# Moving one buffer, sixteen casts and the offsets of a written-out order in a fused attention and expert kernel

## The chip, the cores and the metric

The kernel runs on one core of a Trainium2 chip. The metric is the device time of one execution in microseconds (us). Differences of under 1% are taken as no change in this text.

## The reference

The input is a thresholded attention, a dense feed-forward block and a soft mixture of experts, one after the other. Cut to what matters:

```python
scores = q @ k.T / 8                                  # 4 batches, 8 heads, 576 tokens, head size 64
scores = where(scores >= max(scores) - tau, scores, -1e9)
x = softmax(scores) @ v                               # heads joined: 2304 tokens x 512
g = maximum(x @ w_in, 0) ** 2                         # 2304 x 2048
x = g @ w_out                                         # 2304 x 512
logits = x @ phi                                      # 32 slots
d, c = softmax(logits, axis=0), softmax(logits, axis=1)
s = d.T @ x                                           # 4 slots for each of 8 experts
y[e] = maximum(s[e] @ w1[e], 0) @ w2[e]               # expert width 1024
out = c @ y
```

## The kernel before, in words

**Three bodies of work share the engines.** The attention takes two heads at a time: a pair of heads of one batch is a job, split at first in two, and a job has five query tiles of 128 rows, the last one (mixed) holding the remaining 64 rows of both heads. The weights are converted meanwhile: `w_in` (16 chunks) to two float16 parts, and `w_out` (16 chunks) to 32-bit words that are multiplied with `phi` and stored to memory. The feed-forward runs in nine units of 256 tokens (two for a batch, one for the remainders). After all of it comes a tail with a fixed order: the experts, whose weights are loaded late because their space is that of the attention.

**One query tile.** `s` (TensorE, L688 to L712) makes the scores of two heads; `top` (VectorE, L738) scales them to `u` and takes the bound; `bound` (GpSimd, L744) adds tau; `expo` (ScalarE, L750) makes the exponentials in a tile `e`, both heads in one; `keep` (VectorE, L754) sets what lies below the threshold to zero and sums. In batch 0 and in the mixed tiles TensorE then transposes `e` (`turn`, L275) and ScalarE evacuates it (`p_evac`, L819 and L821). In batches 1 to 3 the full tiles are split in two float16 halves in a tile `hl`: `high` on ScalarE (L773), `low` on GpSimd in four instructions (L777), and a transposing DMA on the SyncE queue (`dturn`, L784) moves `hl` to `pt`. A tile `e` comes free after the last `low` or `turn`, a tile `hl` after its `dturn`. `av` (TensorE, L873 and L881) multiplies with the values.

**One chunk of the weights.** `c_load` brings 128 rows to a slot of `raw64` (eight slots, which later hold q and k of the attention as well). `c_scale` (`head`, L338 on VectorE or L340 on ScalarE) casts the top bytes from bfloat16 to float16; `c_low` (VectorE, L344) makes the low word; `c_shift` (VectorE, L348) joins both and frees the slot. For `w_in` follow a sum of squares, a power of two as the scale, and the halves (`w_hi` L437, `w_lo` L440, `w_times` L445, `w_rest` L450). For `w_out` follow transposes, `c_evac` (L374), `c_prod` (TensorE, L379) and a store. `HDV` says which chunks, by number modulo 4, are cast on VectorE.

**The order is written out by a planner.** `add(kind, engine, cost, ...)` enters each piece with a key; `Plan.run` then plays the kernel through in model time and, on each engine that is free, issues the ready piece of the smallest key. What it issues is the order of the instructions on that engine; an engine later takes them strictly in that order. A key is a due time in planned us (attention and conversion), or 1e5 and a running number (TensorE's pieces of the feed-forward, which therefore fill what the attention leaves), or -1e5 (the feed-forward's pieces on the other engines, which go first). To the key comes an offset for the kind, from `LEAD`. Slots of a buffer are handed out in the order of the keys, too, and the planner knows their number: `EB` of `e`, `HB` of `hl`.

Of the kernel before, what the change touches and what calls it, by code (L numbers as in the profile page):

```python
# [147 lines left out]
def tile_kernel(  # L148
# [31 lines left out]
    RB = 8  # L180
    CB = 4
    GB = 4
    EB = 3
    UB = 4
    PTB = 2
    XPB = 3
    MMB = 4
    QKB = 2
    HB = 2
    WAIT = 0.0  # L190
    DQ = 2.212
    T0 = 10.0
# [4 lines left out]
    TO = 3.4  # L197
    C0 = 2.604
    LOWP = ()
    LEAD = {'c_evac': 8.5, 'c_hi': 109.5, 'c_lo': 76.5, 'c_load': -19.6, 'c_low': 0.2, 'c_out': -17.5, 'c_prod': 65.3, 'c_scale': 13.2, 'c_shift': -19.8, 'c_store': -158.3, 'c_unit': 0.1, 'f_a': 18.2, 'f_acc': 7.3, 'f_alpha': -43.9, 'f_b': -30.4, 'f_cmax': -2.3, 'f_csum': -1.6, 'f_dk': 3.5, 'f_l4': -7.7, 'f_max': 43.7, 'f_merge': 5.1, 'f_p12': -4.1, 'f_pl': 278.3, 'f_pm': -7.7, 'f_relu': 3.3, 'xhi': 3.4, 'xlo': -1.1, 'f_gk': 15.9, 'w_load': 17.8, 'c_turn': 0.0, 'f_sq': -4.5, 'f_p1k': 2.2, 'lphi': -16.2, 'f_turn': 1.5, 'f_p3': -14.5, 'recip': 2.7, 'dturn': -3.1, 'q_scale': -2.9, 'p_evac': -20.3, 'f_total': 0.3, 'w_rest': -1.1, 'av': -1.0, 'r_evac': -3.3, 'w_hi': 6.6, 'w_scale': 0.3, 'v_hi': -6.8, 'top': 3.1, 'eps': -10.6, 'w_diag': -4.8, 'low': -4.3, 'v_scale': -9.2}  # L200
    COST = {('bound', 'POOL'): 0.245, ('c_evac', 'ACT'): 0.493, ('c_low', 'DVE'): 0.35, ('c_low', 'POOL'): 2.12, ('c_out', 'DVE'): 0.104, ('c_scale', 'ACT'): 1.255, ('c_scale', 'DVE'): 0.7, ('c_shift', 'DVE'): 0.61, ('expo', 'ACT'): 0.67, ('f_alpha', 'ACT'): 0.63, ('f_ce', 'ACT'): 0.1, ('f_cmax', 'DVE'): 0.36, ('f_csum', 'DVE'): 0.91, ('f_dk', 'DVE'): 0.22, ('f_gk', 'ACT'): 0.491, ('f_gk', 'DVE'): 0.606, ('f_l4', 'ACT'): 0.279, ('f_max', 'DVE'): 0.33, ('f_merge', 'DVE'): 0.67, ('f_relu', 'ACT'): 0.58, ('f_sq', 'ACT'): 0.525, ('f_sq', 'DVE'): 0.668, ('f_total', 'DVE'): 0.31, ('high', 'ACT'): 0.576, ('keep', 'DVE'): 0.825, ('low', 'POOL'): 0.695, ('q_hi', 'ACT'): 0.73, ('q_lo', 'DVE'): 0.8, ('q_scale', 'DVE'): 0.61, ('q_sq', 'ACT'): 0.82, ('recip', 'DVE'): 0.16, ('spread', 'POOL'): 0.356, ('top', 'DVE'): 0.813, ('v_abs', 'ACT'): 1.2, ('v_hi', 'ACT'): 1.01, ('v_lo', 'DVE'): 1.02, ('w_hi', 'ACT'): 0.612, ('w_lo', 'DVE'): 0.62, ('w_rest', 'POOL'): 1.3, ('w_scale', 'DVE'): 0.6, ('w_sq', 'ACT'): 0.73, ('w_times', 'POOL'): 1.18, ('x_scale', 'DVE'): 0.9, ('xhi', 'ACT'): 0.35, ('xhi', 'DVE'): 0.268, ('xlo', 'DVE'): 0.398}
    PORT = {('w_id', 'POOL'), ('low', 'POOL'), ('w_times', 'POOL'), ('w_rest', 'POOL'), ('spread', 'POOL'), ('c_low', 'POOL'), ('keep', 'DVE'), ('xhi', 'DVE'), ('xlo', 'DVE'), ('c_low', 'DVE'), ('c_shift', 'DVE'), ('w_lo', 'DVE'), ('v_lo', 'DVE'), ('q_lo', 'DVE')}
    FKEY = 1e5
    DTU = (6, 7)
    DEA = (0, 1)
    GKL = (1, 3)
# [5 lines left out]
    DIFD = ()  # L212
    GRAM = True
    QF = 10
    HDV = (0, 2)
    XHA = ()
    QL = 19.2
    LL = 16.0
# [7 lines left out]
    state = {}  # L226
    plan = Plan(
        dict(
            s=1, ma=1, mm=MMB, old=4, u=UB, e=EB, pt=PTB, rp=3, rb=2, rr=2, hl=HB, vh=1, mx=2, xp=XPB, xh=2, xl=1, gt=MC // 2 + 1,
            gk=GB, l4=1, dT=1, qt=QKB, kt=QKB, vraw=2, vbd=2,  # L230
            sm=5, raw64=RB, cv=CB,
        ),
        ("mm", "ma", "xp", "old"),
        WAIT,
        DQ,
    )

    def add(kind, eng, cost, fn, deps=(), key=0.0, *args, **kw):
        cost = COST.get((kind, eng), cost)
        return plan.add(eng, cost, fn, deps, key + LEAD.get(kind, 0.0), *args, port=(kind, eng) in PORT, **kw)  # L240

    def mm_tile(tag="mm"):
        return psp[tag].tile([128, 512], F32, tag=tag, name="mm")
# [722 lines left out]
    def ffn_ops(units):  # L966
# [215 lines left out]

        pending = None
        for n, u in enumerate(units):
            d = dict(gt={}, sq=[], rl=[])
            x = {}
            xdeps = ev_at[u]

            bs = B if u == "rem" else u[0]
            up = scl[:, bs, 1:2]  # L1190

            def xhi(kk, u=u, x=x, up=up):
                if kk == 0:
                    x["x"] = xr if u == "rem" else xp[u]
                    x["h"] = fx.tile([128, KC, NU], F16, tag="xh", name="xh", bufs=2)
                if kk in XHA:
                    nc.scalar.activation(x["h"][:, kk, :], x["x"][:, kk, :], AF.Copy, scale=up)
                else:
                    nc.vector.tensor_scalar(x["h"][:, kk, :], x["x"][:, kk, :], up, None, ALU.mult)

            def xlo(kk, x=x, up=up):
                if kk == 0:
                    x["l"] = fx.tile([128, KC, NU], F16, tag="xl", name="xl", bufs=1)
                nc.vector.scalar_tensor_tensor(
                    x["l"][:, kk, :], x["x"][:, kk, :], up, x["h"][:, kk, :], ALU.mult, ALU.subtract
                )

            hs, ls = [], []
            for kk in range(KC):
                xd = xdeps[kk::KC] + (hs[-1:] if kk else prev.get("hs", [])[-1:] + [xs_op[B if u == "rem" else u[0]]])  # L1210
                h = add("xhi", "ACT" if kk in XHA else "DVE", 0.45 if kk in XHA else 0.2, lambda f=xhi, kk=kk: f(kk), xd, HI, [] if kk else ["xh"])
                l = add("xlo", "DVE", 0.37, lambda f=xlo, kk=kk: f(kk), [h] + ls[:1],
                        HI, [] if kk else ["xl"], [] if u == "rem" else [("xp", xdeps[0])])
                hs.append(h)
                ls.append(l)
            prev["hs"] = hs
            ms = []
            for m2 in range(MC // 2):
                o = {}

                def mm_half(i, m2=m2, x=x, o=o):
                    if i == 0:
                        o["h"] = mm_tile()
                    m = 2 * m2 + i
                    f4, f0 = m * 128 // CW, m * 128 % CW
                    wh, wl = [w_sb[y, f4][:, :, f0:f0 + 128] for y in ("h", "l")]
                    terms = []
                    for kk in range(KC):
                        terms += [(wh[:, kk, :], x["h"][:, kk, :]), (wl[:, kk, :], x["h"][:, kk, :])]
                    for kk in range(KC):  # L1230
                        terms += [(wh[:, kk, :], x["l"][:, kk, :])]
                    for n_, (a, c) in enumerate(terms):
                        nc.tensor.matmul(  # L1233
                            o["h"][:, i * NU:(i + 1) * NU], a, c, start=n_ == 0, stop=n_ == len(terms) - 1
                        )

                f4 = 2 * m2 * 128 // CW
                down = scl[:, bs, 4 + f4:5 + f4]

                def relu(m2=m2, d=d, o=o, down=down):  # L1240
                    g = o["g"] = gt_tile()
                    d.setdefault("pair", {})[m2] = g
                    nc.scalar.activation(g, o["h"], AF.Relu, scale=down)  # L1243
                    d["gt"][2 * m2], d["gt"][2 * m2 + 1] = g[:, 0:NU], g[:, NU:2 * NU]

                def square(m2=m2, o=o, down=down):
                    g = o["g"]
                    if m2 % 4 in SQD:
                        nc.vector.scalar_tensor_tensor(g, o["h"], down, g, ALU.mult, ALU.mult)
                    else:  # L1250
                        nc.scalar.activation(g, g, AF.Square)  # L1251

                a = add("f_a", "PE", 1.31, lambda f=mm_half: f(0), hs + ls + ms[-1:] + (conv_in if n == 0 else []), pk(), ["mm", "gt"])
                b_ = add("f_b", "PE", 1.31, lambda f=mm_half: f(1), [a], pk())
                ms.append(b_)
                dv = m2 % 4 in SQD
                r = add("f_relu", "ACT", 0.49, relu, [b_], HI, [], [] if dv else [("mm", a)])
                s = add("f_sq", "DVE" if dv else "ACT", 0.61 if dv else 0.53, square, [r], HI, rel=[("mm", a)] if dv else [])
                d["rl"].append(a)
                d["sq"].append(s)  # L1260
                if m2 == 0 and pending:
                    pending()
            state["mm"] = ms
            state.setdefault("xl", []).append(ls)
            plan.release(ms[-1], [("xh", hs[0]), ("xl", ls[0])])
            pending = lambda u=u, d=d, n=n: post(u, d, n == 0, n == len(units) - 1, n in DTU)
# [342 lines left out]
```

## Time and profile before

| | before |
|---|---|
| median of 3 runs | 628.82 us (627.69 to 632.64) |
| profiled execution, span from first to last instruction | 624.6 us |
| profiled execution, own time around the span | not recorded by itself; the span is 4.2 us under the median and 3.1 us under the fastest run |
| TensorE busy | 572.8 us (92%) |
| VectorE busy | 449.0 us (72%) |
| ScalarE busy | 447.9 us (72%) |
| GpSimd busy | 286.4 us (46%) |
| DMA moved | 120.97 MB |

PE is TensorE's matmul stream, DVE is VectorE, ACT is ScalarE, POOL is GpSimd and SP is SyncE, whose queue issues nearly all DMAs. L12 is line 12 of the kernel. The shares are means over stages with different limits, so the stages are read one by one.

### The profile page before, as it was taken

To read this page: it belongs to the slowest core of one execution; us is meant where nothing else is said; L and a number is where in the kernel's file an instruction comes from. 1 tells how busy PE (TensorE), PEld (TensorE's weight loads), DVE (VectorE), ACT (ScalarE), POOL (GpSimd) and SP (SyncE) were. 2 spreads that over 40 slices of the span, in tenths; PEclk is the share of its full clock that TensorE was granted. 3 is DMA by queue.
4 is the path that set the end of the run, shared out by engine and by line. 5 is a ranking of instruction groups with operands and counts; after the bars stand their busy time and mean duration, and the time that the engine had idled before them with its cause. 6 is when DMAs were issued, how large, how long until landed. Compare 5 with 4: busy or idle time off the path is not lost. (4 is left out here: it accounts for less than half of the span.)

```text
span 624.6 us, 14082 instructions
## 1 busy us (share of the span) xinstructions
PE 572.8 (92%) x5178; PEld 399.6 (64%) x5178; DVE 449.0 (72%) x1265; ACT 447.9 (72%) x848; POOL 286.4 (46%) x464
## 2 busy tenths in 40 slices
PE   3897979989999999999999989999999999999972
PEld 1454546667677678668757756766777877864321
DVE  5799998999988988887888898878762342342233
ACT  2798666678888988988988878988875857441012
POOL 1455682257667767586756658766750000010000
PEclk9999898999999999999999999999999999999997
DMA  8965525567789676685767655554647799899968
GB/s 274 369 209 189 181 81 186 208 173 202 194 149 195 130 178 108 108 175 123 158 138 138 134 117 104 104 106 95 106 77 233 180 353 225 299 377 387 421 263 302
DMA packets 165940, 120.97 MB, mean 194 GB/s; under 512 B 136560, under 2 KB 145520, under 8 KB 163696
## 3 DMA queue, kind: packets, MB, share of 16 engines
q1 hardware_dynamic: 165296, 117.98, 69.8%
q10 hardware_dynamic: 576, 2.10, 1.1%
q8 instruction: 41, 0.67, 0.4%
q14 instruction: 27, 0.22, 0.1%
HBM read 73.72 MB, written 8.91 MB: 132 GB/s over the span
## 5 line engine op out<-in xcount | busy, mean ns | idle before, releaser
L1233 PEld LDWEIGHTS <-w 128*128 128x128 f16 x1728 | 166.2, 98 | 28.2 <-issue 9.3
L777 POOL TENSOR_TENSOR hl<-e,hl 128x288 f16<-128x288 f32 x192 | 149.2, 800 | 38.0 <-issue 26.8
L1233 PE MATMUL mm<-xh,w 128*128 128x256 f16 x1152 | 149.7, 273 | 0.2 <-ACT gk L1123 0.2
L754 DVE SCALAR_TENSOR_TENSOR e<-u,sm,e 128x576 f32<-128x576 f32 x144 | 122.0, 862 | 18.0 <-ACT e L750 14.4
L750 ACT ACTIVATE e<-u,sm 128x576 f32<-128x576 f32 x144 | 109.2, 771 | 22.1 <-DVE u L738 15.6
L744 POOL TENSOR_SCALAR sm<-sm,tau_p 128x1 f32<-128x1 f32 x144 | 72.8, 511 | 71.9 <-DVE u L738 68.2
L1233 PE MATMUL mm<-xl,w 128*128 128x256 f16 x576 | 86.4, 273 | 0.0
L738 DVE TENSOR_SCALAR_CACHE_REDUCE u<-s,raw 128x576 f32<-128x576 f32 x90 | 71.2, 811 | 13.5 <-PE s L712 12.7
L1243 ACT ACTIVATE gt<-mm,scl 128x512 f32<-128x512 f32 x72 | 49.2, 683 | 42.4 <-PE mm L1233 41.6
L773 ACT ACTIVATE hl<-e 128x576 f16<-128x576 f32 x96 | 64.4, 676 | 2.1 <-DVE e L754 2.0
L841 POOL TENSOR_SCALAR sm<-sm 128x4 f32<-128x4 f32 (+1 forms) x48 | 21.7, 452 | 55.7 <-DVE e L754 47.5
L1251 ACT ACTIVATE gt<-gt 128x512 f32<-128x512 f32 x72 | 45.1, 626 | 1.1
L738 DVE TENSOR_SCALAR_CACHE_REDUCE u<-s,nscale 128x576 f32<-128x576 f32 x54 | 42.6, 808 | 3.4 <-PE s L699 2.8
L1379 POOL MEMSET cv<- 128x512 f32 x4 | 1.9, 525 | 91.2 <-PE mm L1152 91.2
L821 ACT ACTIVATE pt<-mm 128x512 f32<-128x512 f32 x48 | 28.5, 601 | 19.6 <-PE mm L275 19.1
L712 PEld LDWEIGHTS <-qt 128*128 128x128 f16 (+3 forms) x400 | 21.9, 99 | 28.6 <-issue 18.1
L275 PE MATMUL mm<-ident_r,e 128*128 128x128 f32 (+1 forms) x224 | 37.3, 302 | 2.8 <-DVE e L754 2.2
L275 PEld LDWEIGHTS mm<-ident_r,e 128*128 128x128 f32 (+1 forms) x224 | 27.9, 153 | 15.9 <-DVE e L754 5.3
L881 PE MATMUL po<-pt,vh 128*64 128x256 f16 x576 | 36.0, 275 | 0.0
L712 PE MATMUL s<-kt,qt 128*128 128x512 f16 (+1 forms) x200 | 32.9, 289 | 2.4 <-DVE u L738 2.2
L881 PEld LDWEIGHTS <-vh 128*64 128x64 f16 x576 | 29.6, 110 | 5.1 <-issue 4.4
L712 PE MATMUL s<-raw,qt 128*128 128x64 f16 (+1 forms) x200 | 31.2, 293 | 0.0
(205 smaller groups left out, 993.8 us busy)
## 6 DMA issues: line engine op xcount, KB each, us to landing
w<-in_moe_w_dram SPq DMA_DIRECT2D x17, 1024.0 KB, 11.7
w<-in_moe_w_dram SPq DMA_DIRECT2D x22, 512.0 KB, 7.3
raw<-in_moe_w_in_dram SPq DMA_DIRECT2D x16, 511.8 KB, 6.8
raw<-in_moe_w_out_dram SPq DMA_DIRECT2D x16, 511.8 KB, 4.1
raw<-in_v_dram SPq DMA_DIRECT2D x20, 256.0 KB, 3.1
w_out<-cv SPq DMA_DIRECT2D x16, 256.0 KB, 2.7
w<-w_out SPq DMA_DIRECT2D x8, 512.0 KB, 7.9
kt<-in_k_dram SPq DMA_DIRECT2D x10, 320.0 KB, 3.4
```

What stands on the lines that cost most here:

```text
L275: nc.tensor.transpose(out_, in_, ident[:n, :n])
L712: nc.tensor.matmul(o0, d["qh"][r, a, q0], kk, start=full, stop=not full)
L738: nc.vector.tensor_scalar(u, o["s"][:, s0:s0 + S], d.get("nscale", nscale), None, ALU.mult, ALU.min, accum_out=gd["sm"][:, c:c + 1])
L744: nc.gpsimd.tensor_scalar(sm[:, 4 + c:5 + c], sm[:, c:c + 1], tau_p, None, ALU.add)
L750: nc.scalar.activation(e, o["u", a], AF.Exp, scale=-1.0, bias=gd["sm"][:, c:c + 1])
L754: nc.vector.scalar_tensor_tensor(e, o["u", a], sm[:, 4 + c:5 + c], e, ALU.is_le, ALU.mult, accum_out=sm[:, 8 + c:9 + c])
L773: nc.scalar.activation(o["hl"][:, a * S:(a + 1) * S], o["e"][:, a * S:(a + 1) * S], AF.Copy)
L777: nc.gpsimd.tensor_tensor(o["hl"][:, 2 * S:][:, i], o["e"][:, i], o["hl"][:, i], ALU.subtract)
L881: nc.tensor.matmul(po[64 * a:64 * a + 64, :n_], d["vh"][:, y, c0:c0 + D], gd["pt"][:, :, c + 5 * a + m, :], start=i == 0 and m == 0, stop= ...
L1233: nc.tensor.matmul(o["h"][:, i * NU:(i + 1) * NU], a, c, start=n_ == 0, stop=n_ == len(terms) - 1)
L1243: nc.scalar.activation(g, o["h"], AF.Relu, scale=down)
L1251: nc.scalar.activation(g, g, AF.Square)
```

## The change

Four things. The tile `e` has two slots in place of three and the tile `hl` three in place of two (`EB`, `HB`; an `e` is 2 x 576 float32 and an `hl` 4 x 576 float16 for a partition, the same 4,608 bytes). `HDV` becomes empty, so that the 16 casts of chunks 0 and 2 modulo 4 go from VectorE to ScalarE. `LEAD` holds, for each kind, five offsets in place of one: for keys of the attention and conversion the part is chosen by the key (below 40, 76, 140, 270, above), for those of the feed-forward by the unit (0 and 1, 2 and 3, 4 and 5, 6 and 7, 8). And every kind has an entry; before, a kind without one had 0.

```diff
-    EB = 3
+    EB = 2
...
-    HB = 2
+    HB = 3
...
-    LEAD = {..., 'c_load': -19.6, 'c_scale': 13.2, 'c_shift': -19.8, 'c_store': -158.3, 'c_prod': 65.3, 'low': -4.3, 'p_evac': -20.3, 'top': 3.1, 'w_hi': 6.6, 'w_load': 17.8, ...}
+    LEAD = {..., 'bound': (258.1, 112.4, 140.5, 287.5, 198.1), 'c_load': (-21.8, -14.8, -27.8, -22.3, -22.3),
+        'c_prod': (341.5, 355.7, 536.1, 341.5, 341.5), 'c_scale': (365.8, 439.5, 434.8, 428.6, 428.6), 'c_shift': (-136.1, -23.4, -20.8, -18.2, -18.2),
+        'c_store': (-384.9, -310.3, -294.9, -384.9, -384.9), 'expo': (-26.3, -4.4, -3.9, -0.3, -3.9), 'high': (-58.2, -58.2, -169.1, -38, -30.3),
+        'keep': (0.2, -16.5, -41.4, 5.9, -22.1), 'low': (56.7, 56.7, 36.9, -8.9, 9.3), 'p_evac': (-235.8, -169.8, -164.2, -198.9, -211.2),
+        's': (-235.9, -112.8, -100.6, -41.3, 80.4), 'top': (1.6, -0.2, 32.5, 115.1, 230.1), 'turn': (-1.4, 2.4, -1.2, -15.1, -3),
+        'w_hi': (88.2, 213.1, 150.8, 150.8, 150.8), 'w_load': (-150.6, -65.9, -65.9, -65.9, -65.9), ...}
...
+    CUTS = (40.0, 76.0, 140.0, 270.0)
...
-    HDV = (0, 2)
+    HDV = ()
...
     def add(kind, eng, cost, fn, deps=(), key=0.0, *args, **kw):
+        part = state.get("unit", 0) // 2 if abs(key) > FKEY / 2 else sum(key >= c for c in CUTS)
         cost = COST.get((kind, eng), cost)
-        return plan.add(eng, cost, fn, deps, key + LEAD.get(kind, 0.0), *args, port=(kind, eng) in PORT, **kw)
+        return plan.add(eng, cost, fn, deps, key + LEAD[kind][part], *args, port=(kind, eng) in PORT, **kw)
...
         for n, u in enumerate(units):
+            state["unit"] = n
...
                 if m2 == 0 and pending:
+                    state["unit"] = n - 1
                     pending()
+                    state["unit"] = n
```

Of the kinds shown, `bound`, `expo`, `high`, `keep`, `s` and `turn` had no entry before, thus an offset of 0; the diff of `LEAD` is cut to the kinds that the text speaks of.

## Rows read from the trace of the kernel before

**Rows 1.** The page's busy times: engine, busy us (share of span) xinstructions.

```profile
PE 572.8 (92%) x5178; PEld 399.6 (64%) x5178; DVE 449.0 (72%) x1265; ACT 447.9 (72%) x848; POOL 286.4 (46%) x464
```

**Rows 2.** Busy time by stage: stretch, its length, engines (instructions), clock, DMA share, GB/s.

```profile
core 0: us, PE busy (x) PEld busy (x) DVE busy (x) ACT busy (x) POOL busy (x), PEclk, DMA share, GB/s
0.00:16.00 16.00, 5.12 (x22) 2.38 (x22) 9.05 (x25) 4.57 (x4) 2.05 (x8) 1.00 0.88 275
16.00:144.00 128.00, 111.75 (x735) 72.13 (x733) 118.26 (x316) 96.09 (x180) 65.95 (x109) 0.95 0.59 199
144.00:300.00 156.00, 153.01 (x1522) 113.74 (x1522) 132.32 (x379) 137.24 (x268) 105.21 (x171) 1.00 0.74 155
300.00:477.00 177.00, 172.31 (x1763) 126.90 (x1767) 140.33 (x405) 147.91 (x295) 111.30 (x174) 1.00 0.59 115
477.00:560.00 83.00, 83.00 (x771) 64.64 (x772) 28.78 (x86) 50.64 (x79) 1.15 (x3) 1.00 0.95 293
560.00:625.00 65.00, 47.62 (x379) 19.75 (x378) 20.22 (x56) 11.49 (x24) 0.77 (x2) 0.94 0.87 343
```

**Rows 3.** The feed-forward's first matmuls: first and last start of L1233.

```profile
L1233 PEld LDWEIGHTS <-w x1728: 95/98/181, 144.1 to 548.9; 128*128 128x128 f16 x192
```

**Rows 4.** The chain that ended last, near its end: start, us, what.

```profile
566.45 8.87 DMA w<-in_moe_w_dram
...
591.62 13.82 DMA w<-in_moe_w_dram
```

**Rows 5.** The second stage by halves, columns as in Rows 2.

```profile
96.00:144.00 48.00, 44.95 (x342) 31.36 (x340) 45.01 (x124) 35.49 (x69) 19.41 (x36) 0.97 0.62 197
16.00:96.00 80.00, 66.80 (x395) 40.77 (x394) 73.25 (x193) 60.59 (x112) 46.55 (x74) 0.93 0.58 200
```

**Rows 6.** Groups by line from 16 to 144 us: the casts on both engines.

```profile
L338 DVE CAST raw<-raw 128x512 f16<-128x512 bf16 x13 | 12.3, 1004 | 0.0
...
L340 ACT ACTIVATE raw<-raw 128x512 f16<-128x512 bf16 x13 | 17.5, 1367 | 3.9 <-DMA raw<-in_moe_w_in_dram 3.8
```

**Rows 7.** Casts on VectorE, whole run: ns min/median/max, first and last start.

```profile
L338 DVE CAST raw<-raw x16: 716/962/1223, 6.1 to 134.1; 128x512 f16<-128x512 bf16 x16
```

**Rows 8.** One stretch in which both engines are nearly full, columns as in Rows 2.

```profile
32.00:48.00 16.00, 14.56 (x105) 9.15 (x101) 15.96 (x44) 15.26 (x27) 7.52 (x13) 1.00 0.71 226
```

**Rows 9.** ScalarE's waits from 16 to 144 us: total, times, longest.

```profile
ACT pt L821 <- PE mm L275: 14.0, 13, 2.9
ACT e L750 <- DVE u L738: 10.6, 11, 2.6
```

**Rows 10.** SyncE's queue waits from 0 to 144 us.

```profile
SPq L328 <- DVE gt L348: 17.2, 8, 7.0
...
SPq L328 <- DVE cv L348: 10.0, 5, 3.7
```

**Rows 11.** VectorE's waits from 144 to 477 us.

```profile
DVE e L754 <- ACT e L750: 12.7, 13, 2.3
DVE u L738 <- PE s L712: 12.7, 15, 2.4
...
DVE e L754 <- POOL sm L744: 1.4, 2, 1.2
```

**Rows 12.** ScalarE's waits from 144 to 477 us, on a slot of e.

```profile
ACT e L750 <- POOL hl L777: 5.8, 7, 1.2
```

**Rows 13.** The page's group of `high`: count, busy us, mean ns, idle before it.

```profile
L773 ACT ACTIVATE hl<-e 128x576 f16<-128x576 f32 x96 | 64.4, 676 | 2.1 <-DVE e L754 2.0
```

**Rows 14.** Exponentials on ScalarE in order of time, 325 to 338 us.

```profile
325.40 2.11 ACT L750 ACTIVATE e<-u,sm 128x576 f32<-128x576 f32 x3
...
337.80 0.78 ACT L750 ACTIVATE e<-u,sm 128x576 f32<-128x576 f32 x1 [0.89 <-POOL hl L777]
```

**Rows 15.** The low halves on GpSimd that end before that wait does.

```profile
335.83 1.93 POOL L777 TENSOR_TENSOR hl<-e,hl 128x288 f16<-128x288 f32 x2
```

**Rows 16.** Exponentials alone, from 144 to 477 us: ScalarE's busy time (count).

```profile
144.00:477.00 333.00, 76.95 (x102) 1.00 0.66 134
```

More of the change, by code (lines that the diff above doesn't have):

```diff
@@ L199, in tile_kernel @@
     LOWP = ()
-    LEAD = {'c_evac': 8.5, 'c_hi': 109.5, 'c_lo': 76.5, 'c_load': -19.6, 'c_low': 0.2, 'c_out': -17.5, 'c_prod': 65.3, 'c_scale': 13.2, 'c_shift': -19.8, 'c_store': -158.3, 'c_unit': 0.1, 'f_a': 18.2, 'f_acc': 7.3, 'f_alpha': -43.9, 'f_b': -30.4, 'f_cmax': -2.3, 'f_csum': -1.6, 'f_dk': 3.5, 'f_l4': -7.7, 'f_max': 43.7, 'f_merge': 5.1, 'f_p12': -4.1, 'f_pl': 278.3, 'f_pm': -7.7, 'f_relu': 3.3, 'xhi': 3.4, 'xlo': -1.1, 'f_gk': 15.9, 'w_load': 17.8, 'c_turn': 0.0, 'f_sq': -4.5, 'f_p1k': 2.2, 'lphi': -16.2, 'f_turn': 1.5, 'f_p3': -14.5, 'recip': 2.7, 'dturn': -3.1, 'q_scale': -2.9, 'p_evac': -20.3, 'f_total': 0.3, 'w_rest': -1.1, 'av': -1.0, 'r_evac': -3.3, 'w_hi': 6.6, 'w_scale': 0.3, 'v_hi': -6.8, 'top': 3.1, 'eps': -10.6, 'w_diag': -4.8, 'low': -4.3, 'v_scale': -9.2}
+    LEAD = {'av': (-39.9, -201.1, -174.8, -18.8, -189), 'bound': (258.1, 112.4, 140.5, 287.5, 198.1), 'c_evac': (11.5, -89.5, 120.8, 11.5, 11.5), 'c_load': (-21.8, -14.8, -27.8, -22.3, -22.3), 'c_low': (-1.5, 18.7, 133.5, -7.5, -7.5), 'c_out': (-159.4, -327.9, -194.5, -159.4, -159.4), 'c_prod': (341.5, 355.7, 536.1, 341.5, 341.5), 'c_scale': (365.8, 439.5, 434.8, 428.6, 428.6), 'c_shift': (-136.1, -23.4, -20.8, -18.2, -18.2), 'c_store': (-384.9, -310.3, -294.9, -384.9, -384.9), 'c_turn': (231.8, 192.1, 205.8, 231.8, 231.8), 'dturn': (-10.2, -10.2, -4.2, -6.4, 0.7), 'eps': (-626.1, -502.4, -261.4, -393.2, -255.9), 'evac': (-77.1, -19.9, 22, 139.3, -12.1), 'expo': (-26.3, -4.4, -3.9, -0.3, -3.9), 'f_a': (7.8, 6.9, 23.1, 41.2, 89), 'f_acc': (-276.5, -296.9, -213.2, -146.5, -275.4), 'f_alpha': (-602.5, -515.5, -483.8, -422.7, -76.4), 'f_b': (-125.8, -77, -228.2, -133, -296.8), 'f_ce': (-104.1, 31.6, 194.8, -70.2, -51.7), 'f_cmax': (-126.9, -47.4, -46.2, -43.8, -141), 'f_csum': (-234.9, -316.1, -218.1, -318.2, -291), 'f_dk': (-284, -64.4, -203.4, -120, -336.3), 'f_gk': (9.1, 294.1, 275.1, 214, 244.5), 'f_join': (-51.5, -51.5, -51.5, -45.8, -51.5), 'f_l4': (-397.3, -67.8, -66.5, -42.1, -20.2), 'f_max': (-400.7, -191.3, -819.6, -249.3, -148.6), 'f_merge': (-401.4, 1.2, -16.5, -187.8, -104.5), 'f_move': (-140.2, -140.2, -140.2, -27.2, -140.2), 'f_p12': (-118.8, -176.5, -178.2, -109.4, 57.8), 'f_p1k': (-236.9, -89, 29.2, -104.8, -16.8), 'f_p3': (-0.2, -45.9, -83.4, -120.5, -169.1), 'f_part': (114.6, 114.6, 114.6, 67.3, 114.6), 'f_pl': (517.2, 640, 442.6, 609.1, 978.5), 'f_pm': (-145.9, -119.5, -256.7, -269.5, -365.2), 'f_relu': (-579.7, -542.5, -295, -397.7, -407), 'f_rs': (71.6, 71.6, 71.6, 71.6, 71.5), 'f_sq': (-94.2, -365, -232, 26.3, -376.2), 'f_total': (-4, -245.1, -106.5, 40.6, 52.4), 'f_turn': (-2.1, -21.1, -29.4, 1.6, 132.3), 'high': (-58.2, -58.2, -169.1, -38, -30.3), 'keep': (0.2, -16.5, -41.4, 5.9, -22.1), 'low': (56.7, 56.7, 36.9, -8.9, 9.3), 'lphi': (17.6, 136.4, 17.6, 17.6, 17.6), 'lraw': (-4.9, 9.5, -0.4, -15.5, -35.4), 'lrem': (4.1, 8.1, 152.7, 102.3, 8.1), 'p_evac': (-235.8, -169.8, -164.2, -198.9, -211.2), 'q_hi': (5, 5, 25.2, -330.6, -32.6), 'q_lo': (-255.4, -255.4, -344.9, -394, -415.2), 'q_move': (-7.2, -7.2, 3.4, -12, -203.6), 'q_scale': (47.4, 47.4, 121, 60.3, 68.1), 'q_sq': (10.7, 10.7, -7.8, -5.1, 43.9), 'q_sum': (56.2, 56.2, 126.3, 98.1, 189.9), 'r_evac': (-193.2, -7.7, -0.1, -222.8, -338.8), 'r_turn': (0.5, 10.2, 0.6, 0, -14.8), 'recip': (2.8, 23.2, 22.6, 19, 120.7), 's': (-235.9, -112.8, -100.6, -41.3, 80.4), 'spread': (-255, -205.5, -97.5, -72, -87.9), 'top': (1.6, -0.2, 32.5, 115.1, 230.1), 'turn': (-1.4, 2.4, -1.2, -15.1, -3), 'v_abs': (-209.1, -285.9, -263.8, -252.1, -59.2), 'v_hi': (-83.2, -83.2, -187.7, -76.2, -60), 'v_lo': (48.8, 48.8, -23.3, 40.6, -25.8), 'v_scale': (-324.1, 18.8, 167.6, 154.4, -357.5), 'v_sum': (114.3, 33.4, -3.2, -58.2, 105.3), 'w_diag': (-50.6, 57, -133.5, -133.5, -133.5), 'w_diff': (-239.1, 106.3, -87.2, -87.2, -87.2), 'w_gram': (32.9, 167.2, 114.6, 114.6, 114.6), 'w_hi': (88.2, 213.1, 150.8, 150.8, 150.8), 'w_id': (489.7, 302.5, 300.7, 300.7, 300.7), 'w_lo': (1.9, -92, 2.7, 2.7, 2.7), 'w_load': (-150.6, -65.9, -65.9, -65.9, -65.9), 'w_pre': (-38.2, 48.9, 48.9, 48.9, 48.9), 'w_rest': (-152.8, 140.9, -37, -37, -37), 'w_round': (196.1, 340.5, 184.3, 184.3, 184.3), 'w_scale': (-0.3, -21, 2.8, 2.8, 2.8), 'w_sum': (137.6, 169.3, 100.1, 100.1, 100.1), 'w_times': (321.3, 378.5, 230.8, 230.8, 230.8), 'w_wide': (20.4, 20.4, 20.4, 20.4, -133.3), 'x_scale': (-148.5, -136.7, -136.7, -162.1, -151), 'xhi': (107.7, 211.3, 220.4, 267.9, 289.8), 'xlo': (-181.3, -127.3, -13.1, 15.2, 54.9)}
```

## The prediction

> **What bounds the kernel now.** I read the page's busy line first: TensorE is busy for 572.8 of 624.6 us [rows 1]. The change takes no matmul away and adds none, so it can only shorten the roughly 52 us in which TensorE stands idle. The table by stage shows where they are [rows 2]. From 0 to 16 us: 10.9 idle, while the first data arrive. From 16 to 144: 128 - 111.75 = 16.3 idle. From 144 to 477: 333 - 325.3 = 7.7 idle. From 477 to 560: none. From 560 on: 17.4 idle, in a tail whose order is not planned.
>
> The stage from 16 to 144 us has no filler: the feed-forward's first matmul starts at 144.1 [rows 3]. VectorE is full there, 118.26 of 128 us (92%), and ScalarE is not, 96.09 (75%). The halves of that stage say where filler would help: 13.2 us of TensorE's idle time lie before 96 us, 3 after [rows 5]. From 144 to 477 TensorE is 98% busy, VectorE 82% and ScalarE 86% [rows 2]. After the attention, at 477, the expert weights stream in: the DMA share is 0.95 up to 560, and the chain that ended last consists of those loads from 566 to 605 [rows 2, 4]. So an earlier end pays only if the attention ends earlier (its space is then loaded into) and TensorE's work is denser; both move together where the first stage gets shorter.
>
> The sum is made against the profiled execution, span 624.6 us. Its time around the span is not known; the span stands 4.2 us under the median 628.82, and I apply the difference to the median.
>
> **Part 1, the casts.** In the stage from 16 to 144 us VectorE has 13 of them for 12.3 us, and 13 on ScalarE cost 17.5 [rows 6]; the other three of VectorE's 16 lie before 16 us, where both engines wait for data. Moved, VectorE has 118.3 - 12.3 = 106.0 and ScalarE 96.1 + 17.5 = 113.6. The good end: VectorE stays the limit at its share of 92.4%, 106.0 / 0.924 = 114.7, so 13.3 us are gained. The bad end: ScalarE becomes the limit at the best share that it has over a long stage, 137.24 / 156 = 88% [rows 2], so 113.6 / 0.88 = 129.1, a loss of 1.1. Between them lies the one stretch where both are nearly full, with ScalarE at 15.26 of 16 us, 95.4% [rows 8]: 113.6 / 0.954 = 119.1, a gain of 8.9. I take 4, the middle of 8.9 and -1.1, because that stretch is only 16 us long. A cast takes 1.37 us and its key is now 366 to 440 behind its due time, so that any attention piece that is ready goes ahead of it; it has to fit in ScalarE's gaps, and the two largest, waits for a transpose and for `u`, sum to 24.6 us in 24 pieces of at most 2.9 [rows 9]. Thirteen casts need 17.5 of that, but a cast that has begun holds up an exponential by up to 1.37.
>
> The row says that a cast costs 0.95 us as a median on VectorE, up to 1.22, against 1.37 on ScalarE [rows 6, 7]. The Trainium skill, Perfetto Trace Analysis, section Optimizing Scalar/DVE Operations, says that VectorE is the faster one where it has a performance mode, and that moving work to ScalarE may pay when VectorE is saturated. By its first half the stage loses 17.5 - 12.3 = 5.2 us of engine time and the time would be 634; by the second, with VectorE at 92%, it gains the full 13.3. The rows carry both, as ends above and as rivals below.
>
> What is queued behind a late cast: `c_shift` waits for it, and with it the slot of `raw64`. SyncE's queue already stands 27.2 us for such slots [rows 10], and the q, k and v loads are behind those on the queue. The loads' own offsets differ by 2 to 8 us from before, so I cost them at nothing: the feed-forward does not need the weights before 144.
>
> **Part 2, the slots.** No row shows ScalarE idle for a slot of `hl`: `high` has 2.1 us of idle time before it in 96 instructions, 2.0 of them for `keep` [rows 13]. So the third `hl` is worth 0 by itself; at most it lets the planner issue what it held back. The third `e` is used: exponentials wait 5.8 us, 7 times, for the last `low` of an older tile [rows 12]. One such case: the tile whose `low` ends at 335.83 + 1.93 = 337.76 had its first exponential at about 326.8 at the latest (the third of three from 325.40), so it held its slot 11 us [rows 14, 15]. What two slots allow: 102 exponentials from 144 to 477 us [rows 16] are 102 x 80 / 144 = 57 tiles (64 tiles of two heads and 16 of one make 144), one in 333 / 57 = 5.84 us, so two slots do as long as a slot is held for under 11.7 us on average. That is close. Ends: 0, and the rival below. I take 0 loss, because the new offsets shorten the hold: in the later parts `keep` goes before `top` (-41 to 6 against 32 to 230), `high` before `expo`, and `low` before `bound` on GpSimd.
>
> **Part 3, the offsets.** What differs most on TensorE is `s`, which now goes 41 to 236 us ahead of its old place up to key 270. VectorE waits 12.7 us for scores and 12.7 for exponentials between 144 and 477 [rows 11]; earlier scores take from the first. The added wait is `bound` behind up to four `low`, on which `keep` waits; it costs 1.4 us now [rows 11]. Only TensorE's idle 7.7 us can come back here; ends 7.7 and, for a worse fit of the plan to the chip, a loss of the same size. I take a gain of 4, about half, since the scores are the largest of these waits and the work that fills TensorE is unchanged. On SyncE's queue stores of `w_out` go still earlier and `w_load` by 168; the stage that they load in is 95% full, so 0. The first 16 us and the tail: 0; their cover is the data's arrival and the stream of loads.
>
> **Sum.** -4 - 4 = -8 from the span, 616.6, and 621 for the median.
>
> **The rivals.** (a) All comes back: VectorE alone limits the first stage (-13.3) and all of 7.7 us is refilled: 628.8 - 21 = 608. For it: ScalarE's gaps are long enough in sum. Against: they are in 24 pieces, and 95% is the most that it ever shows.
>
> (b) ScalarE takes VectorE's place and the gain is given back: +1.1 and nothing from the offsets, 630. For it: 113.6 us of work in a stage that must then be under 120 long; and the 5.2 us of added engine time, in full and uncovered, would give 634. Against: casts of `w_out` need not be done before 144, and ScalarE has 14% free after that.
>
> (c) The two `e` slots limit the attention between 144 and 477: it decides from a mean hold of 11.7 us. At 12.4, 0.7 above, a tile takes 6.2 us in place of 5.84, so the attention ends 57 x 0.36 = 20 us later. TensorE fills with feed-forward, but the loads start later; of their 128 us from 477 to 605 about 5%, 6 us, are free. The end moves by 14, less the 4 of part 1: 639. For it: the hold of 11 us read above and the waits that three slots already show. Against: `keep`, `high` and `low` now come first.
>
> **How the numbers follow.** My forecast has 0.43, (a) 0.11, (b) 0.25, (c) 0.15; the other 0.06 are mishaps and windfalls that I can't name. The forecast's own range is 612 to 628 (part 1 from 8.9 to 0, part 3 from 7.7 to 0, with something left over). The range from 608 to 637 leaves out the outer half of (a), most of (c) and the unnamed. Within 1% is what a measurement here can't tell from no change: 622.5 to 635.1. Faster by more: 0.36 of the forecast's 0.43, (a) and 0.03, so 0.50. Slower: (c), a fifth of (b) and 0.02, so 0.22. Same: the rest, 0.28.
>
> **What would show it.** Part 1: in the stage before the feed-forward, VectorE loses 12 us, ScalarE gains 17 to 18, and the feed-forward's first matmul starts at about 140 or earlier; if it starts after 144, or ScalarE's share there is above 95% while VectorE's falls under 85%, (b) is right. Part 2: exponentials that wait for `low` for well over 5.8 us in total, and an attention that ends after 477, are (c). Part 3: VectorE's wait for scores falls under 12.7 and TensorE's idle time in the attention stage under 7.7. The forecast is wrong if the first stage is as long as before, or if it is shorter and the loads at the end start no earlier.

## The result and the profile after

The changed kernel takes 612.66 us (median of 4 runs, 610.26 to 613.72) against 628.3 us: a ratio of 0.9743, 95% interval 0.9709 to 0.9778. The forecast was 621, so the direction was right and the gain, 15.6 us, is twice the one forecast. Here and below, medians and ratios leave out disturbed, slower executions.

The profiled execution took 610.26 us with a span of 608.5, so 1.8 us lie around the span. By that the profiled execution of before, span 624.6, stood near 626.4, about 2 us under its median, and not 4.2 as the prediction took it.

First the page's busy times of the changed kernel (columns as in [rows 1]).

```profile
PE 566.6 (93%) x5178; PEld 396.2 (65%) x5178; DVE 437.5 (72%) x1249; ACT 463.4 (76%) x864; POOL 280.6 (46%) x464
```

VectorE lost 11.5 us and ScalarE gained 15.5: in the main the casts. TensorE has the same 5178 matmuls, but is busy for 6.2 us less than in [rows 1]. Its idle time is 608.5 - 566.6 = 41.9 us, against 51.8: so 9.9 us of the 16.1 that the span lost were idle time, and 6.2 are shorter busy time of the same matmuls. The stages of the changed kernel (columns as in [rows 2]):

```profile
0.00:16.00 16.00, 5.45 (x24) 2.70 (x24) 8.06 (x23) 9.22 (x7) 2.06 (x8) 1.00 0.88 299
16.00:96.00 80.00, 73.42 (x499) 47.22 (x498) 76.66 (x212) 77.42 (x139) 46.06 (x73) 1.00 0.71 242
96.00:144.00 48.00, 45.54 (x349) 32.34 (x347) 43.84 (x124) 39.59 (x75) 30.40 (x50) 0.96 0.65 190
144.00:300.00 156.00, 153.24 (x1543) 112.88 (x1542) 132.05 (x376) 136.81 (x269) 100.26 (x170) 1.00 0.73 146
300.00:477.00 177.00, 174.07 (x1763) 130.60 (x1764) 129.89 (x380) 148.69 (x290) 99.91 (x161) 1.00 0.64 132
477.00:560.00 83.00, 82.65 (x762) 56.76 (x763) 32.28 (x98) 42.88 (x72) 1.92 (x4) 1.00 1.01 306
560.00:609.00 49.00, 32.23 (x252) 13.74 (x244) 14.73 (x39) 8.83 (x18) 0.00 (x0) 0.92 0.82 328
```

The row to read is the second, against the second of [rows 5]. From 16 to 96 us TensorE now does 499 matmuls in place of 395 and is idle for 6.6 us in place of 13.2; VectorE is 96% busy (92% before) and ScalarE 97% (76% before). From 144 to 477 TensorE's idle time goes from 7.7 to 5.7 us [rows 2]. TensorE's idle time in the other stages moved by under 1 us each. Next the first feed-forward matmul, and the chain near its end (start, us, what):

```profile
L1237 PEld LDWEIGHTS <-w x1728: 95/98/181, 150.3 to 534.7; 128*128 128x128 f16 x192
```

```profile
559.19 16.23 DMA w<-in_moe_w_dram
575.44 13.81 DMA w<-in_moe_w_dram
```

The feed-forward starts 6 us later than in [rows 3] and ends 14 us earlier (534.7 against 548.9), and the loads at the end of the chain finish at 589.25 and not at 605.44 [rows 4]. The mark that the prediction set, a first feed-forward matmul at 140 or earlier, did not come true: the stage without the feed-forward got 6 us longer, and more attention was done in it. The attention's last matmul starts at 458.3 us, 476.7 before. By 150 us ScalarE had run 49 exponentials, 44 before (one row each, first the changed kernel, the line's instructions from 0 to 150 us; share of DMA and GB/s last):

```profile
0.00:150.00 150.00, 38.11 (x49) 0.99 0.71 230
```

```profile
0.00:150.00 150.00, 33.83 (x44) 0.95 0.64 210
```

The waits that the prediction spoke of, from 144 to 477 us in the changed kernel, VectorE's and then ScalarE's (total, times, longest):

```profile
DVE u L741 <- PE s L715: 13.5, 16, 2.3
...
DVE e L757 <- POOL sm L747: 5.8, 8, 1.4
```

```profile
ACT e L753 <- POOL hl L780: 3.8, 5, 2.3
```

VectorE's wait for scores did not fall (12.7 in [rows 11]); the added wait behind `bound` is there, 5.8 us against 1.4; and exponentials wait less for a slot of `e` with two slots than they did with three (5.8 in [rows 12]).

### The profile page after: what moved, and what is told of

It is laid out like the page before. It is cut to its first block, busy times and chain, and to the rows that moved or that the text cites. A ratio compares the mean times of both kernels' runs of the same rounds, so it can differ in the third digit from the quotient of the medians.

```text
span 608.5 us, 14103 instructions
## 1 busy us (share of the span) xinstructions
PE 566.6 (93%) x5178; PEld 396.2 (65%) x5178; DVE 437.5 (72%) x1249; ACT 463.4 (76%) x864; POOL 280.6 (46%) x464
## 4 chain that ended last, share of the span: by engine, by line
PE 36%; DMA 8%; DVE 7%; ACT 2%; issue 2%; POOL 1%; DVEq 0%; ACTq 0%; POOLq 0%; SPq 0%
PE mm L1237 21%; DMA w<-in_moe_w_dram 8%; PE mm L278 3%; PE s L715 3%; PE po L884 3%; PE mm L990 2%; DVE e L757 2%; PE mm L1155 1%; DVE u L741 1%; POOL hl L780 1%; PE po L889 1%; DVE ob L1529 1%; DVE raw L643 1%; DVE xl L1208 0%; PE mm L997 0%
## 5 line engine op out<-in xcount | busy, mean ns | idle before, releaser
L780 POOL TENSOR_TENSOR hl<-e,hl 128x288 f16<-128x288 f32 x192 | 145.9, 784 | 44.3 <-ACT hl L776 32.7
L757 DVE SCALAR_TENSOR_TENSOR e<-u,sm,e 128x576 f32<-128x576 f32 x144 | 119.3, 849 | 13.8 <-POOL sm L747 8.3
L747 POOL TENSOR_SCALAR sm<-sm,tau_p 128x1 f32<-128x1 f32 x144 | 71.1, 500 | 68.1 <-DVE u L741 64.5
L741 DVE TENSOR_SCALAR_CACHE_REDUCE u<-s,raw 128x576 f32<-128x576 f32 x90 | 71.1, 810 | 13.8 <-PE s L715 13.5
L343 ACT ACTIVATE raw<-raw 128x512 f16<-128x512 bf16 x32 | 42.8, 1388 | 5.6 <-DMA raw<-in_moe_w_in_dram 5.6
L844 POOL TENSOR_SCALAR sm<-sm 128x4 f32<-128x4 f32 (+1 forms) x48 | 19.8, 413 | 40.9 <-DVE e L757 37.7
L278 PEld LDWEIGHTS mm<-ident_r,e 128*128 128x128 f32 (+1 forms) x224 | 25.3, 142 | 18.1 <-issue 6.5
L278 PE MATMUL mm<-ident_r,e 128*128 128x128 f32 (+1 forms) x224 | 34.8, 285 | 2.0 <-DVE e L757 1.2
```

Source lines behind the costliest of these rows:

```text
L278: nc.tensor.transpose(out_, in_, ident[:n, :n])
L741: nc.vector.tensor_scalar(u, o["s"][:, s0:s0 + S], d.get("nscale", nscale), None, ALU.mult, ALU.min, accum_out=gd["sm"][:, c:c + 1])
L747: nc.gpsimd.tensor_scalar(sm[:, 4 + c:5 + c], sm[:, c:c + 1], tau_p, None, ALU.add)
L757: nc.vector.scalar_tensor_tensor(e, o["u", a], sm[:, 4 + c:5 + c], e, ALU.is_le, ALU.mult, accum_out=sm[:, 8 + c:9 + c])
L780: nc.gpsimd.tensor_tensor(o["hl"][:, 2 * S:][:, i], o["e"][:, i], o["hl"][:, i], ALU.subtract)
```

## The experiments

The theories at the start: A, the new offsets make an order that keeps ScalarE and VectorE full at once before 100 us, and the casts and slots only make room for it; B, taking the casts off VectorE is itself the gain; C, the slots are. Each part by itself first.

**Casts alone.**

```diff
  (the kernel before)
-    HDV = (0, 2)
+    HDV = ()
```

> The kernel before with the 16 casts moved to ScalarE, old offsets and old slots, the order planned anew. Theory A (the gain of 16 us is made before 100 us, by an order that keeps ScalarE and VectorE full at once; the casts only make room): within 4 us of the kernel before, 624 to 632, ScalarE's share from 16 to 96 us between 85 and 92%. Theory B (taking the casts off VectorE, the limit, is itself the gain): 616 to 621, with 7 to 11 us gone from the first 100 us. Theory C (the slots make it): no change, 626 to 630.

Measured: 630.26 us, ratio to before 1.0033 (0.9997 to 1.007). No gain. From 16 to 96 us of this run, from 48 to 96, and its page's busy times:

```profile
16.00:96.00 80.00, 70.12 (x446) 44.28 (x447) 73.07 (x202) 76.07 (x133) 46.87 (x78) 0.98 0.66 228
48.00:96.00 48.00, 42.81 (x305) 27.35 (x303) 45.43 (x126) 47.56 (x81) 31.24 (x52) 1.00 0.51 169
PE 580.9 (92%) x5178; PEld 403.0 (64%) x5178; DVE 437.0 (69%) x1249; ACT 464.4 (74%) x864; POOL 279.1 (44%) x464
```

Theory A's time came out; its share did not: from 16 to 96 us ScalarE is 95% busy (99% from 48 on), VectorE 91%. TensorE idles for 9.9 us there (13.2 before), and the feed-forward starts at 141.2 us, 3 us earlier. Over the whole span of 630.7 us its idle time is 49.8, only 2.0 less than before, while its busy time is 8.1 longer, at a clock of 0.973 (0.983 before). So the time is that of rival (b), 630, but (b)'s marks are not there: the feed-forward is not late, and VectorE is not under 85%. The Trainium skill, Perfetto Trace Analysis, section Optimizing Scalar/DVE Operations, holds that moving work to ScalarE may pay when VectorE is saturated; here, at 92%, it did not by itself.

**Slots alone, and both.**

```diff
  (the kernel before; the second run with HDV = () as well)
-    EB = 3
+    EB = 2
-    HB = 2
+    HB = 3
```

> The kernel before with two slots of e and three of hl, old offsets and casts. Theories A and B: 626 to 636, since exponentials then wait longer for a slot (over 5.8 us from 144 to 477). Theory C: 622 or less.

> Both, with the old offsets: the whole change but for the offsets. Theory A: 622 to 634, so that the new offsets are worth at least 10 us. Theory B: 615 to 621. Theory C: under 620.

Measured: 630.72 us, ratio 1.0046 (1.0021 to 1.0071), and 628.06 us, ratio 0.9981 (0.9951 to 1.001). All of the change but the offsets is worth nothing. B and C fall; on top of it the offsets are worth 628.06 - 612.66 = 15.4 us (12.6 by a second measurement of the changed kernel, 615.46 us, at the end of this section). With the slots alone exponentials did not wait longer for a slot of `e`, as A and B had it, but for 3.2 us from 144 to 477 (5.8 in [rows 12]). Where the old offsets leave the early stage, from 16 to 48 and from 48 to 96 us of the run with both:

```profile
16.00:48.00 32.00, 25.86 (x150) 15.51 (x150) 29.40 (x82) 30.15 (x55) 16.23 (x26) 1.00 0.91 326
48.00:96.00 48.00, 41.30 (x279) 27.16 (x280) 41.39 (x115) 44.82 (x76) 26.58 (x46) 0.93 0.50 171
```

TensorE idles for 6.1 and 6.7 us there, 12.8 together, against 6.6 with the new offsets. The new offsets without the casts or with the old slots were not tried: the planner finds no order with them. Three slots of both tiles do not fit the memory.

**The new order, with the casts on VectorE.** The order stays; only the engine of 16 instructions is changed.

```diff
  (the changed kernel)
-                if top == "DVE":
+                if n % 4 in (0, 2):
```

> The changed kernel in its own written-out order, but the 16 casts of chunks 0 and 2 modulo 4 run on VectorE at the place in its queue where the order has them. VectorE gets back about 11 us of work before 96 us, where it is 96% busy, and ScalarE loses 14 to 16 us. Theory A with both engines as limits, and theory B: 8 to 13 us slower than the changed kernel, 620 to 626. If the order alone counts and the engine of a cast does not: 612 to 616.

Measured: 621.16 us, ratio 0.988 (0.9839 to 0.9921). Inside the new order the move of the casts is worth 8.5 us (5.7 against 615.46), inside the old one nothing. The order was planned for the casts on ScalarE; for VectorE the planner finds none with the new offsets. From 16 to 96 us, and to 144:

```profile
16.00:96.00 80.00, 70.13 (x481) 43.93 (x480) 78.34 (x211) 65.09 (x124) 47.72 (x71) 1.00 0.66 230
96.00:144.00 48.00, 42.26 (x305) 29.06 (x305) 45.99 (x126) 34.75 (x65) 28.91 (x44) 0.97 0.64 199
```

VectorE is 98% full, ScalarE 81%, and TensorE idles for 9.9 and 5.7 us where the changed kernel has 6.6 and 2.5: one full engine sets the pace as long as the other is not used.

**Which offsets.** Theory A1: the conversion's, with the casts going last. A2: the attention's own. One group put back to the old values in each run, and in the third the casts' alone.

```diff
  (the changed kernel; three runs)
-    LEAD = {...}
+    LEAD = {..., every kind c_*, w_* and lphi: its one old offset five times}   # first
+    LEAD = {..., every kind of the attention: its one old offset five times}    # second
+    LEAD = {..., 'c_scale': (13.2, 13.2, 13.2, 13.2, 13.2)}                     # third
```

> The changed kernel with the old offsets for the kinds of the weights' conversion (c_ and w_, and phi's load), the new ones for attention and feed-forward. Theory A1 (what fills ScalarE and VectorE early is that the conversion, the casts above all, goes last and fits in gaps): 622 to 630. Theory A2 (the attention's own new offsets, scores first and finished tiles first, make it): 612 to 617.

> The changed kernel with the old offsets for the attention's kinds, the new ones for conversion and feed-forward. Theory A1: 612 to 618. Theory A2: 622 to 632. If neither works without the other: over 620 here and over 620 with the old offsets of the conversion.

> The changed kernel with one offset undone, that of the casts (13.2 as before, in place of 366 to 440), so that a cast goes when it is due and not behind all attention. Theory A1 in its narrow form (the casts' place at the end of ScalarE's choice): 618 to 626, with exponentials later in the first 100 us. If the casts' place does not count: 611 to 615.

Measured: 635.97 us, ratio 1.0144 (1.0119 to 1.0169); 626.02 us, ratio 0.9974 (0.9948 to 1.0001); 632.87 us, ratio 1.0105 (1.0057 to 1.0152). Each takes the whole gain away; the first and the third are slower than any theory here had them. In the first TensorE's idle time is 60.9 us (51.8 before), in the third it is 52.3, as before, and the run's clock is 0.972. That neither group works without the other is what the expectation named for it, but one kind's offset costing as much as a whole group is suspect: it may be that any touch does it.

**Any touch.** All large differences between kinds stay; every offset but those of eight kinds (`top`, `keep`, `turn` and five others) is shifted at random by up to 1 us (twice) and by up to 3.

```diff
  (the changed kernel)
-    LEAD = {..., 'c_scale': (365.8, 439.5, ...), ...}
+    LEAD = {..., each value + uniform(-1, 1) or uniform(-3, 3), ...}
```

> The changed kernel with every offset (but for eight kinds with which the planner finds no order) shifted by a random amount of up to 1 us, which leaves all the large differences between kinds as they are, but gives another written-out order. Theory P (the gain is in what the offsets say on the whole: casts last, scores first): 611 to 618. Theory O (the gain belongs to the one order that these offsets happen to give): 620 to 640, like the runs in which one group of offsets was undone.

> The same with other random shifts of up to 1 us, to see the spread between such orders. Theory P: 611 to 618. Theory O: 620 to 640, and more than 4 us away from the first.

> The same with random shifts of up to 3 us. Theory P: 611 to 620, no farther off than with 1 us. Theory O: 620 to 640, no better and no worse than with 1 us, since any shift gives just another order.

Measured: ratios 0.999 (0.9936 to 1.0043), 1.0003 (0.9972 to 1.0034) and 1.0038 (1.0005 to 1.0071), with medians 626.71, 628.36 and 629.65 us. The gain is gone in all three, with 3 us no more than with 1. (The second is 1.7 us from the first, where theory O expected over 4.) The clock is not the reason: TensorE's idle time is 53.4, 52.0 and 51.8 us, against 41.9; and at clocks of 0.984 to 0.987 four executions of the first took 624.9 to 626.7 us, the changed kernel at 0.983 to 0.986 took 612.4 to 613.7. So theory P falls and O is left: in these three orders, what the offsets say on the whole (casts last, scores first) is worth nothing by itself; the gain belongs to the one order that the changed kernel's values give. And the runs that undid one group say less than they seem to, since a shift that means nothing costs as much. From 16 to 96 us the first two of the three are between before and after, with TensorE idle for 8.9 and 9.1 us:

```profile
16.00:96.00 80.00, 71.10 (x474) 44.50 (x473) 74.24 (x203) 74.40 (x134) 45.55 (x78) 0.98 0.62 214
16.00:96.00 80.00, 70.86 (x472) 44.98 (x472) 74.10 (x211) 77.28 (x138) 41.10 (x72) 0.94 0.67 226
```

**The third slot of hl.** Once planned with two, once with the order of the changed kernel kept and only two slots in memory.

```diff
  (the changed kernel, planned anew)
-    HB = 3
+    HB = 2
  (the changed kernel, same order)
-                        o["hl"] = at.tile([128, 4 * S], F16, tag="hl", name="hl", bufs=HB)
+                        o["hl"] = at.tile([128, 4 * S], F16, tag="hl", name="hl", bufs=2)
```

> The changed kernel with two slots of hl in place of three, two of e, order planned anew. By the prediction's part 2 (no row shows anything waiting for a slot of hl): 611 to 615. If the third slot is what the new order lives on between 144 and 460 us: over 617, with the attention's end later than 458 us.

> The changed kernel in its own order, planned with three slots of hl, but with only two in memory, so that a tile's halves wait for the transposing DMA of the tile two before. If nothing waits for a slot of hl, as part 2 of the prediction had it: 611 to 615. If the third slot carries the new order between 144 and 460 us: over 618, with ScalarE waiting there in front of the first half (L776) for that DMA, and the attention's end later than 458 us.

Measured: 646.83 us, ratio 1.0315 (1.0289 to 1.0342), and 637.1 us, ratio 1.0122 (1.0059 to 1.0184). In the same order the slot is worth 637.1 - 612.66 = 24 us (21.6 against 615.46). In the profiles TensorE's idle time is 15.7 us longer, 57.6 against 41.9, and its busy time 12.8, at a clock of 0.970 against 0.991. The first halves of this run, with what ScalarE waits for in front of them, and its stage from 144 us:

```profile
  DMA pt<-hl: 27.8, 12
```

```profile
144.00:300.00 156.00, 142.92 (x1326) 103.63 (x1326) 116.50 (x326) 120.09 (x236) 86.92 (x149) 0.93 0.62 129
```

ScalarE stands 27.8 us, 12 times, until the transposing DMA has freed a slot; TensorE is idle for 13.1 us there where the changed kernel has 2.8. In [rows 13] nothing waits for a slot: the planner issues a first half only when a slot is free in its own time (`fits`), so the old order, planned with two, holds it back. The run planned anew with two shows it: its first halves wait for a slot for only 2.3 us, and it is the slowest of all. (Both runs have four slots of `e` and `hl` together, the kernel before five.) Both runs have the changed kernel's early stage (TensorE idles for 6.5 and 7.2 us from 16 to 96 us), and their attention's last matmul starts at 499.0 and 487.4 us: the early stage alone does not make the gain.

**Where in the order.** The order is kept up to a planned time, and from there all offsets (again but for eight kinds) are shifted by up to 1 us (other random values in each run), so that another order follows; the third run is the changed kernel beside them.

```diff
  (the changed kernel, in Plan.run)
+            if self.now >= 150.0 and not getattr(self, 'moved', False):   # or 320.0
+                self.moved = True
+                ...   # each piece that is not issued yet gets its key with the shifted offset
```

> The changed kernel's order up to planned 150 us; from there every offset (but for eight kinds) shifted by up to 1 us, so that another order follows. Theory E (the gain is made before 150 us, where 6 heads more are done and 7 us of idle time are gone): it is kept, 611 to 617. Theory W (the order has to fit to the end, an early lead is lost again in the attention's later part): 620 to 630, with the same first 150 us as the changed kernel and the attention ending after 460 us.

> The same with the order kept up to planned 320 us. Theory E: 611 to 617. Theory W: between the changed kernel and the run kept to 150, 614 to 624, with the loss after 320 us alone.

> The changed kernel itself, for a comparison on the same chip: 610 to 615 by every theory, 2 to 3% under the kernel before.

Measured: kept to 150, 622.36 us, ratio 0.9893 (0.9862 to 0.9924); kept to 320, 616.12 us, ratio 0.9804 (0.9747 to 0.986); the changed kernel 615.46 us, ratio 0.9784 (0.9734 to 0.9834). The runs of before beside them have 628.9. So of 13.4 us, 6.5 are left with the order kept to 150 us and 12.8 with it kept to 320: half, and nearly all. E falls; both times lie where W had them. From 300 to 460 us of the run kept to 150, of the one kept to 320, and of the kernel before:

```profile
300.00:460.00 160.00, 150.95 (x1490) 111.27 (x1488) 124.99 (x366) 130.81 (x262) 97.06 (x164) 0.96 0.61 115
```

```profile
300.00:460.00 160.00, 155.99 (x1574) 114.67 (x1572) 128.38 (x382) 135.86 (x275) 100.06 (x164) 0.99 0.61 117
```

```profile
300.00:460.00 160.00, 155.53 (x1571) 114.38 (x1572) 132.69 (x382) 136.32 (x271) 105.39 (x167) 1.00 0.61 118
```

TensorE's idle time is 9.1 us in the first, 4.0 in the second and 4.5 before. So a part of the early lead is lost again there when the order changes at 150: the idle time of that run's whole span is 48.5 us, 3.3 less than before, though 6.4 had been saved by 144 us. The second half needs its own good order. Each rests on one set of shifts; other sets could land elsewhere.

## Why the prediction was right and wrong

**The step that failed is part 3, the offsets.** It said: "Only TensorE's idle 7.7 us can come back here", that is between 144 and 477 us, and took 4. Measured, the offsets are worth 15.4 us with casts and slots in place (12.6 by the second measurement), and most of the idle time that came back lies where part 3 did not look: TensorE's idle time fell by 6.6 us from 16 to 96 and by only 2.0 from 144 to 477, and without the new offsets those 6.6 are not there (12.8 us idle against 13.2). Its reason failed too: the wait for scores went from 12.7 to 13.5 us, and in the three shifted runs the direction of the offsets alone did nothing.

**Part 1, the casts, was wrong in its size.** It took 4 for the casts by themselves; alone they gave no time that can be told from none (630.26 us), and 2 us of idle time. The bound that limited ScalarE to 95.4% at best was too low: in the new order it is 97% busy over 80 us. The casts count with the order: 8.5 us go when they are taken back out of the new order. Its marks misled as well. From 16 to 144 us VectorE did not lose 12 us but was filled with other work (120.5 us, 118.3 before). By the feed-forward's start, 150.3 us, the forecast's own sign of being wrong and one of rival (b)'s signs came true, while the gain was twice the forecast: a start that moves says little where the order decides what is done before it. What held is that the end moves with the loads behind the attention: they finish 16.2 us earlier, and the span is 16.1 shorter.

**Part 2, the slots, was wrong on hl.** "The third `hl` is worth 0 by itself" holds in the old order (the slots alone gave a ratio of 1.0046) and fails in the new one, where it carries 24 us. The step that failed is from "nothing waits for it" to "worth 0": a planned order shows no wait for a resource that it was planned around. On `e` it was right: rival (c) did not come, and the waits fell.

**A step left out.** "It can only shorten the roughly 52 us in which TensorE stands idle" held only for the idle time, 9.9 us against the 8 forecast. The other 6.2 us of the span are TensorE's busy time, and most of them go with the clock. The profiled run of the changed kernel had a mean granted clock of 0.991, before 0.983. A second profile of the changed kernel, at 0.980, has a span of 613.6 us, and its page says:

```profile
PE 571.4 (93%) x5178; PEld 400.2 (65%) x5178; DVE 437.9 (71%) x1249; ACT 463.5 (76%) x864; POOL 279.4 (46%) x464
```

Its idle time is 613.6 - 571.4 = 42.2 us, as in the first; its matmuls took 4.8 us longer. Against before, with nearly the same clock, the span is 11.0 us shorter, 9.6 of it idle time. The profile of before was about 2 us under its own median, so that the medians differ by more. That the clock makes only a small part of the gain is shown by executions of one clock beside each other: at 0.980 the changed kernel had spans of 613.6 to 613.9 us, and the kernel before 626.9 and 627.7. How much of the clock comes with the order stays open: over all runs here, the changed kernel has a mean of 0.984 (8 runs) and before 0.981 (76 runs).

**The sum.** The idle time in all, 9.9 us, came out near the 8 of the forecast by luck, for the terms did not: 4, 0 and 4 were taken for casts, slots and offsets. By themselves the first two give nothing, and the offsets, with the others in place, 15.4 us of time.

What stays open: why this order is the good one, beyond that it keeps VectorE and ScalarE at 96 and 97% before 96 us and TensorE's idle time low after. Shares nearly as high, 93 and 97%, stand in the second shifted order, which has no gain, so they are not shown to be the cause. No single rule in it was shown to carry the gain.

## What to carry to other kernels

Where a planner writes out the order, an engine's or a buffer's worth is that of the order built on it: test a part inside the new order, without changing the order, and not only in the old one. A trace without a wait for a buffer does not say that one more buffer is worth nothing, since the plan may have held the work back. And before an offset is explained, shift all of them by an amount that means nothing: if that takes the gain away, the gain belongs to the one order and not to the reason.

## What the runs showed of the hardware

The same order of the same kernel was granted different clocks in different executions. From 80 to 100 us of the changed kernel in its first profile, and in its second (columns as in [rows 2]):

```profile
80.00:100.00 20.00, 18.24 (x137) 12.84 (x138) 19.68 (x61) 19.88 (x32) 9.33 (x16) 1.00 0.70 235
```

```profile
80.00:100.00 20.00, 18.95 (x132) 13.29 (x133) 19.68 (x59) 19.37 (x31) 9.41 (x16) 0.91 0.67 231
```

1.00 is 2.4 GHz throughout, and 0.91 a stretch in which part ran at 1.2. In the 20 us before them TensorE was busy for 17.7 us in both, at 1.00, so the rows do not say what made it fall. The four runs of the changed kernel behind the result order by it: spans of 608.5, 610.6, 611.2 and 611.9 us at mean clocks of 0.991, 0.986, 0.985 and 0.983, some 4 us for 0.01.

Orders of the same 5178 matmuls were granted different clocks on one chip, too: a mean of 0.981 in 25 executions of the kernel before, and of 0.971 in ten of each of the last two shifted orders, though TensorE's idle time is nearly the same in the profiles of all three (51.8, 52.0 and 51.8 us).
